# Decode attention with heads in quads: three 64 KB ring tiles, V in 64 KB descriptors, wo in 4 KB descriptors

## The chip, the cores and the metric

The kernel runs on one core of one Trainium2 chip. The metric is the device time of one execution in microseconds. It was 667.13 us before (median of 3 runs, 666.98 to 667.53). On one core an execution counts as slow when it is over 1.5% above the fastest of its kernel. The profile's span (first to last instruction on the core) is about 1.8 us shorter than the device time.

## The reference, cut to what matters

A batch of two rows, each with one token. Attention has 32 heads over a cache of 8192 positions with 128 elements, and a small gated MLP follows.

```python
B, Sq, D = 2, 1, 512
Hq, Hkv, Sk, Dh = 32, 32, 8192, 128          # all bfloat16
q = (layernorm(x) @ wq).reshape(B, Sq, Hq, Dh)
p = softmax(einsum(q, k_cache) * Dh ** -0.5)
h = x + einsum(p, v_cache).reshape(B, Sq, Hq * Dh) @ wo
# the MLP (F = 1376): layernorm(h), W_gate, W_up, relu(gate) * up, W_down
out = h + mlp(layernorm(h))
```

K and V are 134 MB each. With wq, wo and the MLP's weights 281 MB must come from HBM, each byte once.

## The kernel before

It takes two heads at a time (a pair). A partition holds 128 positions of one head, so one K or V tile of a pair has rows of 32 KB, and a ring of six such tiles (buffers used in turn) holds K, V and the weights. VectorE (DVE) multiplies K by q and folds the 128 products to a score; ScalarE (ACT) takes the exponential into `pm`; TensorE (PE) multiplies `pm` with V.

```python
ring = ctx.enter_context(tc.tile_pool(name="ring", bufs=6))
...
def load(cache, n, cuts=(0, T2)):                 # T2 = 128 positions per partition
    b, i = seq[n]
    src = cache[b, 2 * i:2 * i + 2].rearrange("h s d -> (h s) d").rearrange(
        "(p t) d -> p t d", p=P)
    t = ring.tile([P, T2, Dh], bf16, tag="s", name="kv")
    for lo, hi in zip(cuts[:-1], cuts[1:]):
        nc.sync.dma_start(out=t[:, lo:hi, :], in_=src[:, lo:hi, :])
    return t
...
def scores(n, between=None):
    ...
    nc.vector.tensor_tensor(out=kt, in0=kt, in1=qb, op=ALU.mult)             # L177
    while width > 8:                                                          # 128 -> 8
        nc.vector.tensor_tensor(out=..., in0=..., in1=..., op=ALU.add)        # L183
    nc.vector.tensor_reduce(out=sc, ...)                                      # L191
    for half in range(2):
        nc.scalar.activation(out=pm[ps, :, half], in_=sc[ps, :], func=ACT.Exp, ...)
...
load_k(0)
for n in range(N - 2):                            # N = 32 pairs
    load_k(n + 1)
    load_v(n)
    scores(n, between=first_row if n == NP + 2 else None)
    ...
    weighted_v_moving(n)

load_k(N - 1)
wo_sb = ring.tile([P, Hq, D], bf16, tag="s")
nc.sync.dma_start(out=wo_sb, in_=A_wo.rearrange("(h d) n -> d h n", d=P))    # 1 KB rows
load_v(N - 2)
CUTS = (0, T2 // 2, T2 * 7 // 8, T2)
load_v(N - 1, CUTS)
...                                               # gate, up and down weights follow, last of all
```

The softmax here doesn't subtract the row's maximum and nothing guards it: scores larger than these inputs give would overflow.

## Time and profile before

| before | |
|---|---|
| device time | 667.13 us |
| DMA queue q1 | 99.1% of 16 engines' span |
| DVE busy | 90% |
| PE busy | 50% |
| DVE waiting for K | 26.9 us |

The page of the profile, kernel before. Part 1 is busy time by engine. In part 2 the span is cut into 40 slices: DMA is the busy share in tenths, GB/s what was moved. Then come the queue (part 3), the chain that ended last (part 4), and the two costliest groups (part 5: line, engine, operation, shapes, count, busy us, mean ns, idle time before them and its cause).

```profile
span 665.2 us, 4281 instructions
PE 335.7 (50%) x1806; PEld 148.1 (22%) x1806; DVE 597.6 (90%) x224; ACT 51.2 (8%) x171; POOL 1.8 (0%) x12
...
DMA  9999999999999999999999999999999999999996
GB/s 378 439 421 433 439 424 429 437 430 424 437 435 420 437 432 422 437 433 427 431 437 423 432 435 432 427 437 428 427 437 426 430 434 431 426 438 421 376 410 242
...
q1 hardware_dynamic: 15368, 281.06, 99.1%
...
DMA 53%; DVE 44%; issue 1%; PE 1%; SPq 0%; DVEq 0%
...
L177 DVE TENSOR_TENSOR kv<-kv,qrep 128x16384 bf16<-128x16384 bf16 x32 | 278.0, 8689 | 26.9 <-DMA kv<-in_A_k_cache_dram 26.9
L183 DVE TENSOR_TENSOR kv<-kv 128x8192 bf16<-128x8192 bf16 (+3 forms) x128 | 276.2, 2158 | 4.3
```

The queue is hardly ever idle: no slice but the last is below 90%. The chain gives DVE 44%, which by itself leaves open which of the two is the bound: in the first third (from 23 to 210 us) the chain runs over DVE because K has already landed when DVE comes to it. DVE needs 18.7 us for a pair (8.69 + 8.7 of folds + 1.22, and the small gaps between them), DMA about 19.4 us, so DVE has 4% to spare.

The next line is from the DMA view of the kernel before, cut to the stretch from 620 to 626 us, in which nothing but wo moves, in 1 KB packets.

```profile
DMA packets 2038, 2.09 MB, mean 348 GB/s; under 512 B 0, under 2 KB 2038, under 8 KB 2038
```

348 GB/s is 20% below the 430 of the K and V stretches. The packet records of the trace say why. A packet in these records has the size of one contiguous run of its DMA (wq and the rows of K and V, all but the last V, are 8192 packets of 32768 bytes), and a median of 16 of them are in flight, as many as the engines by which the page counts; "descriptor", the word of the title, stands here for one such run. These are median durations over all packets of a size; the column "left over" takes off bytes x 0.03674 ns (the slope from 16 to 32 KB, 27.2 bytes per ns, 435 GB/s on 16 engines).

| packet, bytes | median ns | left over, ns |
|---|---|---|
| 1024 | 49 | 11 |
| 2048 | 84 | 9 |
| 2752 | 113 | 12 |
| 4096 | 162 | 12 |
| 12288 | 464 | 13 |
| 16384 | 614 | 12 |
| 32768 | 1216 | 12 |

By these records a packet has a fixed cost: about 12 ns are left over at every size of the table (9 at 2 KB, of which there are only 128 packets). (Packets of 1 KB overlap a little, as q1's share of 108.9% in that view shows, so that their real rate, 348 GB/s, is somewhat better than the 334 that 49 ns gives.)

### The profile page before, as it was taken

How to read it: one execution, taken by the hardware profiler on the slowest of the kernel's cores; microseconds unless marked ns; L12 is line 12 of the kernel's file. 1: busy time of each engine (PE TensorE's matmuls, PEld its weight loads, DVE VectorE, ACT ScalarE, POOL GpSimd, SP SyncE). 2: the span in 40 equal slices, each digit the busy share in tenths (PEclk: the TensorE clock that was granted, in tenths of full speed). 3: DMA queues.
4: the chain of work that ended last, by engine and by line, in shares of the span. 5: the costliest groups of instructions: out<-in, count | busy, mean ns of one | idle time of the engine just before them, and what ended most of it. 6: DMA issues, size and time to landing. Idle time of an engine off the chain costs nothing.

```text
span 665.2 us, 4281 instructions
## 1 busy us (share of the span) xinstructions
PE 335.7 (50%) x1806; PEld 148.1 (22%) x1806; DVE 597.6 (90%) x224; ACT 51.2 (8%) x171; POOL 1.8 (0%) x12
## 2 busy tenths in 40 slices
PE   3343455654446655444565444556653456654345
PEld 2111122211212221121222111222221122211244
DVE  1699999999999999999999999999999998999931
ACT  2200000000000000000000000000000000000000
POOL 1000000000000000000000000000000000000000
PEclk9757878765787776668877666787666777666755
DMA  9999999999999999999999999999999999999996
GB/s 378 439 421 433 439 424 429 437 430 424 437 435 420 437 432 422 437 433 427 431 437 423 432 435 432 427 437 428 427 437 426 430 434 431 426 438 421 376 410 242
DMA packets 15399, 281.33 MB, mean 423 GB/s; under 512 B 1202, under 2 KB 5396, under 8 KB 6932
## 3 DMA queue, kind: packets, MB, share of 16 engines
q1 hardware_dynamic: 15368, 281.06, 99.1%
q8 instruction: 14, 0.23, 0.1%
q14 instruction: 5, 0.04, 0.0%
q10 hardware_dynamic: 12, 0.00, 0.0%
HBM read 281.05 MB, written 0.00 MB: 422 GB/s over the span
## 4 chain that ended last, share of the span: by engine, by line
DMA 53%; DVE 44%; issue 1%; PE 1%; SPq 0%; DVEq 0%
DMA kv<-in_A_k_cache_dram 45%; DVE kv L183 21%; DVE kv L177 21%; DMA kv<-in_A_v_cache_dram 6%; DVE sc L191 3%; DMA wd_sb<-in_B_W_down_dram 2%; PE o_a L223 1%; SPq L266 0%; PE y_ps L351 0%; SPq L95 0%; PE yt_ps L359 0%; DVEq L191 0%; DVE y_row L362 0%; DVE zi_229 L232 0%; DVE oc L236 0%
## 5 line engine op out<-in xcount | busy, mean ns | idle before, releaser
L177 DVE TENSOR_TENSOR kv<-kv,qrep 128x16384 bf16<-128x16384 bf16 x32 | 278.0, 8689 | 26.9 <-DMA kv<-in_A_k_cache_dram 26.9
L183 DVE TENSOR_TENSOR kv<-kv 128x8192 bf16<-128x8192 bf16 (+3 forms) x128 | 276.2, 2158 | 4.3
L211 PE MATMUL o<-kv,pm_85 128*8 128x512 bf16 x320 | 94.0, 466 | 97.9 <-DMA kv<-in_A_v_cache_dram 77.1
L211 PE MATMUL o<-kv,pm_87 128*8 128x512 bf16 x320 | 91.3, 456 | 87.4 <-DMA kv<-in_A_v_cache_dram 87.4
L211 PE MATMUL o<-kv,pm_86 128*8 128x512 bf16 x320 | 90.2, 452 | 83.6 <-DMA kv<-in_A_v_cache_dram 83.6
L211 PEld LDWEIGHTS <-pm_85 128*8 128x8 bf16 x320 | 32.1, 101 | 156.0 <-issue 102.1
L211 PEld LDWEIGHTS <-pm_87 128*8 128x8 bf16 x320 | 31.7, 99 | 142.8 <-issue 105.4
L211 PEld LDWEIGHTS <-pm_86 128*8 128x8 bf16 x320 | 31.6, 99 | 138.0 <-issue 97.0
L215 ACT ACTIVATE osb<-o 8x512 f32<-8x512 f32 x30 | 17.6, 586 | 498.1 <-PE o L211 498.1
L191 DVE TENSOR_REDUCE sc<-kv 128x128 f32<-128x1024 bf16 x32 | 39.0, 1220 | 3.9 <-DVE kv L183 1.0
L217 PE MATMUL ob_226<-sel,osb 8*128 8x2 f32 x128 | 16.8, 248 | 11.8 <-ACT osb L215 11.8
L217 PE MATMUL ob_227<-sel,osb 8*128 8x2 f32 x112 | 14.7, 249 | 10.3 <-ACT osb L215 10.3
L217 PEld LDWEIGHTS ob_226<-sel,osb 8*128 8x128 f32 x128 | 15.4, 186 | 19.9 <-ACT osb L215 18.6
L217 PEld LDWEIGHTS ob_227<-sel,osb 8*128 8x128 f32 x112 | 13.5, 186 | 17.4 <-ACT osb L215 17.4
L145 PE MATMUL qps<-wq_sb,xnb 128*64 128x512 bf16 x64 | 8.6, 433 | 4.7 <-DMA wq_sb<-in_A_wq_dram 4.7
L196 ACT ACTIVATE pm_86<-sc 64x128 bf16<-64x128 f32 x22 | 7.6, 345 | 33.6 <-DVE sc L191 33.3
L196 ACT ACTIVATE pm_85<-sc 64x128 bf16<-64x128 f32 x22 | 7.6, 344 | 28.8 <-DVE sc L191 28.5
L277 PE MATMUL a_ps<-oc,wo_sb 128*128 128x2 bf16 x128 | 3.9, 165 | 10.7 <-DMA wo_sb<-in_A_wo_dram 10.5
L223 PEld LDWEIGHTS <-kv 128*128 128x128 bf16 x256 | 7.1, 104 | 4.4 <-DMA kv<-in_A_v_cache_dram 4.4
L196 ACT ACTIVATE pm_87<-sc 64x128 bf16<-64x128 f32 x20 | 6.9, 345 | 12.8 <-DVE sc L191 12.4
L145 PEld LDWEIGHTS <-xnb 128*64 128x64 bf16 x64 | 5.0, 122 | 7.9 <-issue 4.7
L236 DVE SCALAR_TENSOR_TENSOR oc<-o_b,zi_230 128x2 bf16<-128x2 f32 x1 | 0.2, 161 | 6.8 <-PE o_b L223 6.8
(73 smaller groups left out, 57.0 us busy)
## 6 DMA issues: line engine op xcount, KB each, us to landing
kv<-in_A_k_cache_dram SPq DMA_DIRECT2D x32, 4096.0 KB, 39.5
kv<-in_A_v_cache_dram SPq DMA_DIRECT2D x31, 4096.0 KB, 48.7
wq_sb<-in_A_wq_dram SPq DMA_DIRECT2D x1, 4096.0 KB, 12.3
wo_sb<-in_A_wo_dram SPq DMA_DIRECT2D x1, 4096.0 KB, 50.8
kv<-in_A_v_cache_dram SPq DMA_DIRECT2D x1, 2048.0 KB, 20.8
kv<-in_A_v_cache_dram SPq DMA_DIRECT2D x1, 1536.0 KB
wgu<-in_B_W_gate_dram SPq DMA_DIRECT2D x1, 1376.0 KB, 27.5
wgu<-in_B_W_up_dram SPq DMA_DIRECT2D x1, 1376.0 KB, 30.6
```

Of the source, the lines that this page charges most:

```text
L145: nc.tensor.matmul(out=qps[half * HALF:(half + 1) * HALF], lhsT=xnb[:, c, b, :], rhs=wq_v[:, c, g * QP:(g + 1) * QP, half, :], start=(c == ...
L177: nc.vector.tensor_tensor(out=kt, in0=kt, in1=qb, op=ALU.mult)
L183: nc.vector.tensor_tensor(out=_view(kt, 0, [[Dh, T2], [1, half]]), in0=_view(kt, 0, [[Dh, T2], [1, half]]), in1=_view(kt, half, [[Dh, T2], ...
L191: nc.vector.tensor_reduce(out=sc, in_=_view(kt, 0, [[Dh, T2], [1, 8]]), axis=AXIS.X, op=ALU.add)
L196: nc.scalar.activation(out=pm[ps, :, half], in_=sc[ps, :], func=ACT.Exp, accum_out=zm[ps, b, i, half:half + 1], scale=SCALE)
L211: nc.tensor.matmul(out=o, lhsT=pm[:, ts, :].rearrange("p t two -> p (t two)"), rhs=vt[:, ts, :].rearrange("p t d -> p (t d)"), start=(g == ...
L215: nc.scalar.activation(out=osb, in_=o, func=ACT.Copy)
L217: nc.tensor.matmul(out=ob[b][:, i, :], lhsT=osb[:, j, :], rhs=sel[:, j, :], start=(j == 0), stop=(j == TG - 1))
L223: nc.tensor.matmul(out=o, lhsT=vt[:, t, :], rhs=pm[:, t, :], start=(t == 0), stop=(t == T2 - 1))
L236: nc.vector.scalar_tensor_tensor(out=oc[:, s:e, :, b], in0=o, scalar=1.0 / D, in1=zi[b][:, s:e, :], op0=ALU.mult, op1=ALU.mult)
L277: nc.tensor.matmul(out=a_ps[:, c, :], lhsT=wo_sb[:, h, c * P:(c + 1) * P], rhs=oc[:, h // 2, h % 2, :], start=(h == 0 and c == 0), stop=(h ...
```

## The change

The intent is larger descriptors for the same bytes. Four heads (a quad) share a tile of 64 KB per partition; V comes in one DMA with 64 KB rows. K still comes in two halves of 32 KB rows, so that DVE can begin with the first. The ring becomes three tiles of twice the size. A head now lies over 32 partitions. The order of wo's rows is also changed: (i p j) with four neighbouring rows on one partition gives 4 KB runs, but then o must have that order too. So o is replicated over partitions by a matmul, and a mask with a sum over the free axis picks each partition's four elements (`gather`). The last quad keeps the old order, and 1 KB rows of wo. The output is turned to two rows and sent in one DMA.

```diff
-    NP = Hq // 2
-    T2 = 2 * Sk // P
+    G = 4
+    NQ = Hq // G
+    T = G * Sk // P
+    J = 4
-    ring = ctx.enter_context(tc.tile_pool(name="ring", bufs=6))
+    ring = ctx.enter_context(tc.tile_pool(name="ring", bufs=3))
...
     def load_k(n):
-        kts[n] = load(A_k_cache, n)
+        kts[n] = load(A_k_cache, n, (0, HT, T))
-    def load_v(n, *cuts):
+    def load_v(n, cuts=(0, T)):
...
-        for half in range(2):
-            ps = slice(half * HALF, (half + 1) * HALF)
-            nc.scalar.activation(out=pm[ps, :, half], ...)
+        for h in range(G):
+            ps = slice(h * Q, (h + 1) * Q)
+            nc.scalar.activation(out=pm[ps, lo:hi, h], ...)
...
+    def gather(s, e):
+        r = reps[s // HQ][:, 0:e - s, :]
+        nc.vector.tensor_tensor(out=r.rearrange("p i (m j) -> p i m j", j=J), in0=...,
+                                in1=_view(pick, 0, [[0, e - s], [1, Q], [0, J]]), op=ALU.mult)
+        nc.vector.tensor_reduce(out=ou[:, s:e, :],
+                                in_=r.rearrange("p i (m j) -> p i j m", j=J), ...)
...
     load_k(0)
-    for n in range(N - 2):
+    load_v(0)
+    for n in range(N - 1):
         load_k(n + 1)
-        load_v(n)
-        scores(n, between=first_row if n == NP + 2 else None)
+        scores(n, 0, 0, HT, between.get(n))
+        scores(n, 1, HT, T)
+        if n < N - 3:
+            load_v(n + 1)
+        elif n == N - 3:
+            load_v(n + 1, (0, HT, T))
+        ret = weighted_v(n)
...
-    nc.sync.dma_start(out=wo_sb, in_=A_wo.rearrange("(h d) n -> d h n", d=P))
+    nc.sync.dma_start(out=wo_sb.rearrange("p i j n -> p i (j n)"),
+                      in_=A_wo[0:LQ * G * Dh, :].rearrange("(i p j) n -> p i (j n)", p=P, j=J))
+    nc.sync.dma_start(out=wol, in_=A_wo[LQ * G * Dh:, :].rearrange("(h d) n -> d h n", d=P))
...
-    for b, eng in zip(range(B), (nc.sync, nc.scalar)):
-        eng.dma_start(out=out[b].rearrange("s (c m) -> (s c) m", c=KC), in_=y_row[b:P:Q, :])
+    nc.vector.tensor_copy(y_row[:, 0:D // 2], yt_ps[:, 0:D // 2])
+    nc.scalar.activation(out=y_row[:, D // 2:], in_=yt_ps[:, D // 2:], func=ACT.Copy)
+    nc.sync.dma_start(out=out.rearrange("b s d -> (b s) d"), in_=y_row)
```

More of the change, by code (lines that the diff above doesn't have):

```diff
@@ L38 @@
     KC = D // P
-    NP = Hq // 2
-    T2 = 2 * Sk // P
+    G = 4
+    NQ = Hq // G
+    T = G * Sk // P
+    J = 4
     TG = 4
-    HALF = P // 2
     EPS = 1e-5
@@ L50 @@
     LASTW = F - FULL
-    NM = 3
-    Q = P // KC
+    NM = 2
+    Q = P // G
     ENG = mybir.EngineType
-    assert Sq == 1 and Hkv == Hq and D == KC * P and Hq % 8 == 0 and P == Dh
+    assert Sq == 1 and Hkv == Hq and D == KC * P and Hq % (2 * G) == 0 and T % 32 == 0 and P == Dh
     consts = ctx.enter_context(tc.tile_pool(name="consts", bufs=1))
     misc = ctx.enter_context(tc.tile_pool(name="misc", bufs=1))
-    ring = ctx.enter_context(tc.tile_pool(name="ring", bufs=6))
+    ring = ctx.enter_context(tc.tile_pool(name="ring", bufs=3))
     spool = ctx.enter_context(tc.tile_pool(name="spool", bufs=2))
@@ L67 @@
     mean_f = consts.tile([P, P], f32)
-    zm = consts.tile([P, B, NP, 2], f32)
+    zm = consts.tile([P, B, 3, NQ - 1], f32)
+    zl = consts.tile([P, B, 3, G], f32)
     eps_t = consts.tile([P, 1], f32)
-    pms = [consts.tile([P, T2, 2], bf16, name=f"pm{i}") for i in range(NM)]
-    sel = consts.tile([2 * TG, TG, 2], f32)
+    pms = [consts.tile([P, T, G], bf16, name=f"pm{i}") for i in range(NM)]
     nc.vector.memset(eps_t, EPS)
@@ L74 @@
     nc.vector.memset(zm, 0.0)
+    nc.vector.memset(zl, 0.0)
     for pm in pms:
         nc.gpsimd.memset(pm, 0.0)
-    y = consts.tile([P, KC, Q], bf16)
-    nc.gpsimd.memset(y, 0.0)
     ident = consts.tile([P, P], bf16)
     masks.make_identity(nc, ident)
-    nc.gpsimd.memset(sel, 0.0)
-    nc.gpsimd.affine_select(out=sel, in_=sel, compare_op=ALU.not_equal, fill=1.0, base=0,
-                            pattern=[[-2, TG], [-1, 2]], channel_multiplier=1)
+    head_of = consts.tile([G * TG, G, Q], f32)
+    nc.gpsimd.memset(head_of, 0.0)
+    for t in range(TG):
+        nc.gpsimd.affine_select(out=head_of, in_=head_of, compare_op=ALU.not_equal, fill=1.0,
+                                base=-G * t, pattern=[[-1, G], [0, Q]], channel_multiplier=1)
+    turn_of = consts.tile([G * TG, TG], f32)
+    nc.gpsimd.memset(turn_of, 1.0)
+    same = consts.tile([P, G, Q], f32)
+    nc.gpsimd.memset(same, 1.0)
+    for t, pat, n in ((turn_of, [[G, TG]], G), (same, [[Q, G], [0, Q]], Q)):
+        neg = [[-s_, c_] for s_, c_ in pat]
+        nc.gpsimd.affine_select(out=t, in_=t, compare_op=ALU.is_ge, fill=0.0, base=0,
+                                pattern=neg, channel_multiplier=1)
+        nc.gpsimd.affine_select(out=t, in_=t, compare_op=ALU.is_ge, fill=0.0, base=n - 1,
+                                pattern=pat, channel_multiplier=-1)
+    pick = consts.tile([P, Q], f32)
+    nc.vector.tensor_reduce(out=pick, in_=ident.rearrange("p (h m) -> p m h", h=G),
+                            axis=AXIS.X, op=ALU.add)
     ctx.enter_context(tc.manual_schedule(engines={ENG.PE, ENG.DVE, ENG.Activation, ENG.SP}))
@@ L93 @@
     nc.scalar.dma_start(out=x_row, in_=A_x.rearrange("b s d -> (b s) d"))
-    wq_sb = ring.tile([P, KC, Hq * Dh], bf16, tag="s")
+    RING = T * Dh
+    wq_sb = ring.tile([P, RING], bf16, tag="s", name="wq_sb")[:, 0:KC * Hq * Dh].rearrange(
+        "p (c n) -> p c n", c=KC)
     nc.sync.dma_start(out=wq_sb, in_=A_wq.rearrange("(p c) n -> p c n", p=P))
@@ L131, with load @@
                             op=ALU.mult)
-    xnb = opool.tile([P, KC, B, HALF], bf16, tag="row")
-    nc.vector.tensor_copy(xnb, xn.unsqueeze(3).to_broadcast([P, KC, B, HALF]))
+    xnb = opool.tile([P, KC, B, Q], bf16, tag="row")
+    nc.vector.tensor_copy(xnb, xn.unsqueeze(3).to_broadcast([P, KC, B, Q]))
     nc.scalar.activation(out=warm, in_=xn[0:1, 0, 0:1], func=ACT.Exp)
-    qrep = consts.tile([P, B, NP, Dh], bf16)
+    qrep = consts.tile([P, B, NQ, Dh], bf16)
     QP = 4
-    wq_v = wq_sb.rearrange("p c (i two d) -> p c i two d", two=2, d=Dh)
+    wq_v = wq_sb.rearrange("p c (i h d) -> p c i h d", h=G, d=Dh)
     for b in range(B):
-        for g in range(NP // QP):
+        for g in range(0, NQ, QP):
             qps = ps_mm.tile([P, QP, Dh], f32, tag="mm", name="qps")
-            for half in range(2):
+            for h in range(G):
                 for c in range(KC):
                     nc.tensor.matmul(
-                        out=qps[half * HALF:(half + 1) * HALF],
+                        out=qps[h * Q:(h + 1) * Q],
                         lhsT=xnb[:, c, b, :],
-                        rhs=wq_v[:, c, g * QP:(g + 1) * QP, half, :],
+                        rhs=wq_v[:, c, g:g + QP, h, :],
                         start=(c == 0), stop=(c == KC - 1),
                     )
-            nc.scalar.activation(out=qrep[:, b, g * QP:(g + 1) * QP, :], in_=qps, func=ACT.Copy)
-    seq = [(b, i) for b in range(B) for i in range(NP)]
+            nc.scalar.activation(out=qrep[:, b, g:g + QP, :], in_=qps, func=ACT.Copy)
+    seq = [(b, i) for b in range(B) for i in range(NQ)]
     N = len(seq)
+    HT = T // 2
+    LQ = NQ - 1
     kts, vts = {}, {}
-    def load(cache, n, cuts=(0, T2)):
+    def load(cache, n, cuts):
         b, i = seq[n]
-        src = cache[b, 2 * i:2 * i + 2].rearrange("h s d -> (h s) d").rearrange(
+        src = cache[b, G * i:G * i + G].rearrange("h s d -> (h s) d").rearrange(
             "(p t) d -> p t d", p=P)
-        t = ring.tile([P, T2, Dh], bf16, tag="s", name="kv")
+        t = ring.tile([P, T, Dh], bf16, tag="s", name="kv")
         for lo, hi in zip(cuts[:-1], cuts[1:]):
@@ L167, in load_k, with scores @@
     def load_k(n):
-        kts[n] = load(A_k_cache, n)
-    def load_v(n, *cuts):
-        vts[n] = load(A_v_cache, n, *cuts)
-    def scores(n, between=None):
+        kts[n] = load(A_k_cache, n, (0, HT, T))
+    def load_v(n, cuts=(0, T)):
+        vts[n] = load(A_v_cache, n, cuts)
+    def scores(n, k, lo, hi, between=None):
         b, i = seq[n]
-        kt = kts.pop(n)
-        qb = _view(qrep[:, b, i, :], 0, [[0, T2], [1, Dh]])
-        nc.vector.tensor_tensor(out=kt, in0=kt, in1=qb, op=ALU.mult)
+        kt, w = kts[n], hi - lo
+        off = lo * Dh
+        nc.vector.tensor_tensor(out=kt[:, lo:hi, :], in0=kt[:, lo:hi, :],
+                                in1=_view(qrep[:, b, i, :], 0, [[0, w], [1, Dh]]), op=ALU.mult)
         if between is not None:
@@ L183, in scores @@
             nc.vector.tensor_tensor(
-                out=_view(kt, 0, [[Dh, T2], [1, half]]),
-                in0=_view(kt, 0, [[Dh, T2], [1, half]]),
-                in1=_view(kt, half, [[Dh, T2], [1, half]]),
+                out=_view(kt, off, [[Dh, w], [1, half]]),
+                in0=_view(kt, off, [[Dh, w], [1, half]]),
+                in1=_view(kt, off + half, [[Dh, w], [1, half]]),
                 op=ALU.add,
@@ L189, in scores @@
             width = half
-        sc = spool.tile([P, T2], f32, name="sc")
-        nc.vector.tensor_reduce(out=sc, in_=_view(kt, 0, [[Dh, T2], [1, 8]]),
+        sc = spool.tile([P, HT], f32, name="sc")
+        nc.vector.tensor_reduce(out=sc[:, 0:w], in_=_view(kt, off, [[Dh, w], [1, 8]]),
                                 axis=AXIS.X, op=ALU.add)
         pm = pms[n % NM]
-        for half in range(2):
-            ps = slice(half * HALF, (half + 1) * HALF)
-            nc.scalar.activation(out=pm[ps, :, half], in_=sc[ps, :], func=ACT.Exp,
-                                 accum_out=zm[ps, b, i, half:half + 1], scale=SCALE)
@@ L200 @@
-    ob = [ps_acc.tile([P, NP, 2], f32, name=f"ob{b}") for b in range(B)]
-    oc = misc.tile([P, NP, 2, B], bf16)
-    zi = [misc.tile([P, NP, 2], f32, name=f"zi{b}") for b in range(B)]
-    def weighted_v_moving(n):
-        b, i = seq[n]
-        vt, pm = vts.pop(n), pms[n % NM]
-        o = ps_o.tile([2 * TG, TG, Dh], f32, tag="o", name="o")
-        for g in range(T2 // TG):
-            ts = slice(g * TG, (g + 1) * TG)
-            nc.tensor.matmul(out=o, lhsT=pm[:, ts, :].rearrange("p t two -> p (t two)"),
-                             rhs=vt[:, ts, :].rearrange("p t d -> p (t d)"),
-                             start=(g == 0), stop=(g == T2 // TG - 1))
-        osb = opool.tile([2 * TG, TG, Dh], f32, tag="row", name="osb")
-        nc.scalar.activation(out=osb, in_=o, func=ACT.Copy)
-        for j in range(TG):
-            nc.tensor.matmul(out=ob[b][:, i, :], lhsT=osb[:, j, :], rhs=sel[:, j, :],
-                             start=(j == 0), stop=(j == TG - 1))
@@ L220, in weighted_v_stationary @@
-    def weighted_v_stationary(n, o, lo, hi):
+        for h in range(G):
+            ps = slice(h * Q, (h + 1) * Q)
+            nc.scalar.activation(out=pm[ps, lo:hi, h], in_=sc[ps, 0:w], func=ACT.Exp,
+                                 accum_out=(zm[ps, b, k, i:i + 1] if i < LQ
+                                            else zl[ps, b, k, h:h + 1]), scale=SCALE)
+    oc = misc.tile([P, LQ, J, B], bf16)
+    ol = misc.tile([P, G, B], bf16)
+    HQ = NQ // 2
+    ou = misc.tile([P, LQ, J], f32)
@@ new lines, with v_moving, weighted_v @@
+    reps = {}
+    def v_moving(n, o, lo, hi):
+        vt, pm = vts[n], pms[n % NM]
+        for t in range(lo, hi, TG):
+            ts = slice(t, t + TG)
+            nc.tensor.matmul(out=o, lhsT=pm[:, ts, :].rearrange("p t h -> p (t h)"),
+                             rhs=vt[:, ts, :].rearrange("p t d -> p (t d)"),
+                             start=(t == 0), stop=(t == T - TG))
+    def weighted_v(n):
+        b, i = seq[n]
+        o = ps_o.tile([G * TG, TG, Dh], f32, tag="o", name="o")
+        v_moving(n, o, 0, T)
+        osb = opool.tile([G * TG, TG, Dh], f32, tag="row", name="osb")
+        for t in range(TG):
+            nc.scalar.activation(out=osb[:, t, :], in_=o[:, t, :], func=ACT.Copy,
+                                 scale=turn_of[:, t:t + 1])
+        if i == LQ:
+            o_l = ps_s.tile([P, G], f32, tag="st", name="o_l")
+            for t in range(TG):
+                nc.tensor.matmul(out=o_l, lhsT=osb[:, t, :], rhs=head_of[:, :, 0],
+                                 start=(t == 0), stop=(t == TG - 1))
+            ol_f = misc.tile([P, G], f32)
+            nc.scalar.activation(out=ol_f, in_=o_l, func=ACT.Copy)
+            return ol_f
+        if i % HQ == 0:
+            reps[i // HQ] = ps_acc.tile([P, HQ, Dh], f32, tag=f"rep{i // HQ}", name="rep")
+        for t in range(TG):
+            nc.tensor.matmul(out=reps[i // HQ][:, i % HQ, :],
+                             lhsT=head_of.rearrange("k h m -> k (h m)"), rhs=osb[:, t, :],
+                             start=(t == 0), stop=(t == TG - 1))
@@ new lines, in gather @@
+    def gather(s, e):
+        r = reps[s // HQ][:, 0:e - s, :]
+        nc.vector.tensor_tensor(out=r.rearrange("p i (m j) -> p i m j", j=J),
+                                in0=r.rearrange("p i (m j) -> p i m j", j=J),
+                                in1=_view(pick, 0, [[0, e - s], [1, Q], [0, J]]), op=ALU.mult)
+        nc.vector.tensor_reduce(out=ou[:, s:e, :],
+                                in_=r.rearrange("p i (m j) -> p i j m", j=J),
+                                axis=AXIS.X, op=ALU.add)
@@ L221, in weighted_v_stationary, with v_stationary @@
+    def v_stationary(n, o, lo, hi):
         vt, pm = vts[n], pms[n % NM]
@@ L223, in weighted_v_stationary @@
             nc.tensor.matmul(out=o, lhsT=vt[:, t, :], rhs=pm[:, t, :],
-                             start=(t == 0), stop=(t == T2 - 1))
-    def sum_z(b, s, e):
-        zb = ps_s.tile([P, e - s, 2], f32, tag="st", name="zb")
-        nc.tensor.matmul(out=zb, lhsT=mean_f, rhs=zm[:, b, s:e, :], start=True, stop=True)
-        return zb
-    def inverse_z(b, s, e, zb=None):
-        nc.vector.reciprocal(out=zi[b][:, s:e, :], in_=zb or sum_z(b, s, e))
-    def normalize(b, s, e, o):
-        nc.vector.scalar_tensor_tensor(out=oc[:, s:e, :, b], in0=o, scalar=1.0 / D,
-                                       in1=zi[b][:, s:e, :], op0=ALU.mult, op1=ALU.mult)
@@ L239, in first_row, with sum_z, row_z, last_z @@
-    def first_row():
-        inverse_z(0, 0, NP, zb0)
-        normalize(0, 0, NP, ob[0])
+                             start=(t == 0), stop=(t == T - 1))
+    def sum_z(zb, lhsT, z):
+        for k in range(3):
+            nc.tensor.matmul(out=zb, lhsT=lhsT, rhs=z[:, k, :], start=(k == 0), stop=(k == 2))
+        return zb
+    def row_z(b, zb):
+        return sum_z(zb, same.rearrange("p h m -> p (h m)"), zm[:, b])
+    def last_z(b, zb):
+        return sum_z(zb, mean_f, zl[:, b])
+    def z_tile():
+        return ps_s.tile([P, LQ + G], f32, tag="st", name="zb")
@@ new lines, in normalize, with invert_last, normalize_last @@
+    def normalize(b, zb):
+        zi = misc.tile([P, LQ], f32, name=f"zi{b}")
+        nc.vector.reciprocal(out=zi, in_=zb)
+        nc.vector.tensor_tensor(out=oc[:, :, :, b], in0=ou,
+                                in1=zi.unsqueeze(2).to_broadcast([P, LQ, J]), op=ALU.mult)
+    def invert_last(b, zb):
+        zi = misc.tile([P, G], f32, name=f"zil{b}")
+        nc.vector.reciprocal(out=zi, in_=zb)
+        return zi
+    def normalize_last(b, o, zi):
+        nc.vector.scalar_tensor_tensor(out=ol[:, :, b], in0=o, scalar=1.0 / D,
+                                       in1=zi, op0=ALU.mult, op1=ALU.mult)
@@ L243 @@
+    def first_row():
+        gather(HQ, LQ)
+        normalize(0, zb0)
+        zil = invert_last(0, zl0)
+        normalize_last(0, ol_f, zil)
+    between = {HQ + 1: lambda: gather(0, HQ), NQ + 1: first_row,
+               NQ + HQ + 1: lambda: gather(0, HQ)}
     load_k(0)
-    for n in range(N - 2):
+    load_v(0)
+    for n in range(N - 1):
         load_k(n + 1)
-        load_v(n)
-        scores(n, between=first_row if n == NP + 2 else None)
-        if n == NP + 1:
-            zb0 = sum_z(0, 0, NP)
-        weighted_v_moving(n)
@@ L253 @@
-    load_k(N - 1)
-    wo_sb = ring.tile([P, Hq, D], bf16, tag="s")
-    nc.sync.dma_start(out=wo_sb, in_=A_wo.rearrange("(h d) n -> d h n", d=P))
-    load_v(N - 2)
-    CUTS = (0, T2 // 2, T2 * 7 // 8, T2)
+        scores(n, 0, 0, HT, between.get(n))
[5 more added lines that the diff above has]
+        ret = weighted_v(n)
+        if n == NQ - 1:
+            ol_f = ret
+            z0 = z_tile()
+            zb0, zl0 = row_z(0, z0[:, 0:LQ]), last_z(0, z0[:, LQ:])
@@ new lines @@
+    W = ring.tile([P, RING], bf16, tag="s", name="W")
+    wo_sb = W[:, 0:LQ * J * D].rearrange("p (i j n) -> p i j n", j=J, n=D)
+    at = LQ * J * D
+    wol = W[:, at:at + G * D].rearrange("p (h n) -> p h n", n=D)
+    at += G * D
+    wgu = W[:, at:at + 2 * KC * F].rearrange("p (g c n) -> p g c n", c=KC, n=F)
+    at += 2 * KC * F
+    wd_sb = W[:, at:at + NF * D].rearrange("p (f n) -> p f n", n=D)
+    nc.sync.dma_start(out=wo_sb.rearrange("p i j n -> p i (j n)"),
+                      in_=A_wo[0:LQ * G * Dh, :].rearrange("(i p j) n -> p i (j n)", p=P, j=J))
@@ L258 @@
+    nc.sync.dma_start(out=wol, in_=A_wo[LQ * G * Dh:, :].rearrange("(h d) n -> d h n", d=P))
+    CUTS = (0, HT, T * 13 // 16, T * 15 // 16, T)
     load_v(N - 1, CUTS)
-    wgu = ring.tile([P, 2, KC, F], bf16, tag="s")
     for g, w in enumerate((B_W_gate, B_W_up)):
         nc.sync.dma_start(out=wgu[:, g], in_=w.rearrange("(c p) n -> p c n", p=P))
-    wd_sb = ring.tile([P, FC, D], bf16, tag="s")
+    wd_l = misc.tile([P, D], bf16)
     blocks = [(f, min(4, NF - f)) for f in range(0, NF, 4)]
@@ L268, with project @@
             in_=B_W_down[f * P:(f + r) * P, :].rearrange("(p r) n -> p (r n)", r=r))
-    nc.sync.dma_start(out=wd_sb[0:LASTW, NF, :], in_=B_W_down[FULL:F, :])
+    nc.sync.dma_start(out=wd_l[0:LASTW, :], in_=B_W_down[FULL:F, :])
     a_ps = ps_acc.tile([P, KC, B], f32)
-    def project_o(s, e):
-        for h in range(2 * s, 2 * e):
-            for c in range(KC):
-                nc.tensor.matmul(
-                    out=a_ps[:, c, :], lhsT=wo_sb[:, h, c * P:(c + 1) * P],
-                    rhs=oc[:, h // 2, h % 2, :],
-                    start=(h == 0 and c == 0), stop=(h == Hq - 1),
-                    skip_group_check=True,
-                )
+    def project(w, o, first=False, last=False):
+        for c in range(KC):
+            nc.tensor.matmul(out=a_ps[:, c, :], lhsT=w[:, c * P:(c + 1) * P], rhs=o,
+                             start=(first and c == 0), stop=last, skip_group_check=True)
     L = B - 1
-    scores(N - 2)
+    zb1 = row_z(L, z_tile()[:, 0:LQ])
     def most_of_last_row():
-        inverse_z(L, 0, NP - 1)
-        normalize(L, 0, NP - 2, ob[L][:, 0:NP - 2, :])
-    scores(N - 1, between=most_of_last_row)
-    project_o(0, NP - 2)
-    zb1 = sum_z(L, NP - 1, NP)
-    inverse_z(L, NP - 1, NP, zb1)
-    o_a = ps_o.tile([P, 1, 2], f32, tag="o", name="o_a")
-    weighted_v_stationary(N - 2, o_a[:, 0, :], 0, T2)
-    normalize(L, NP - 2, NP - 1, o_a)
-    o_b = ps_o.tile([P, 1, 2], f32, tag="o", name="o_b")
-    weighted_v_stationary(N - 1, o_b[:, 0, :], CUTS[0], CUTS[1])
-    project_o(NP - 2, NP - 1)
-    for lo, hi in zip(CUTS[1:-1], CUTS[2:]):
-        weighted_v_stationary(N - 1, o_b[:, 0, :], lo, hi)
-    normalize(L, NP - 1, NP, o_b)
-    project_o(NP - 1, NP)
+        gather(HQ, LQ)
+        normalize(L, zb1)
+    scores(N - 1, 0, 0, HT)
+    scores(N - 1, 1, HT, CUTS[2], most_of_last_row)
+    scores(N - 1, 2, CUTS[2], T)
+    for i in range(LQ):
+        for j in range(J):
+            project(wo_sb[:, i, j, :], oc[:, i, j, :], first=(i == 0 and j == 0))
+    o_b = ps_o.tile([P, G], f32, tag="o", name="o_b")
+    v_stationary(N - 1, o_b, 0, CUTS[2])
+    zil = invert_last(L, last_z(L, z_tile()[:, 0:G]))
+    v_stationary(N - 1, o_b, CUTS[2], T)
+    normalize_last(L, o_b, zil)
+    for h in range(G):
+        project(wol[:, h, :], ol[:, h, :], last=(h == G - 1))
     hc = misc.tile([P, KC, B], f32)
@@ L350 @@
         for c in range(KC):
-            nc.tensor.matmul(out=y_ps[:, c, :], lhsT=wd_sb[0:w, fc, c * P:(c + 1) * P],
+            nc.tensor.matmul(out=y_ps[:, c, :], lhsT=(wd_sb[:, fc] if fc < NF else wd_l[0:w])[:, c * P:(c + 1) * P],
                              rhs=act[0:w, fc, :],
@@ L354 @@
                              skip_group_check=True)
-    nc.vector.tensor_tensor(out=y[:, :, 0:B], in0=y_ps, in1=hc, op=ALU.add)
-    yt_ps = ps_o.tile([P, P], f32, tag="o")
+    y = misc.tile([P, KC, B], bf16)
+    nc.vector.tensor_tensor(out=y, in0=y_ps, in1=hc, op=ALU.add)
+    yt_ps = ps_o.tile([B, D], f32, tag="o")
     for c in range(KC):
-        nc.tensor.matmul(out=yt_ps[c * Q:(c + 1) * Q, :], lhsT=y[:, c, :], rhs=ident,
-                         start=True, stop=True, skip_group_check=True)
-    y_row = misc.tile([P, P], bf16)
-    nc.vector.tensor_copy(y_row, yt_ps)
-    for b, eng in zip(range(B), (nc.sync, nc.scalar)):
-        eng.dma_start(out=out[b].rearrange("s (c m) -> (s c) m", c=KC), in_=y_row[b:P:Q, :])
+        nc.tensor.matmul(out=yt_ps[:, c * P:(c + 1) * P], lhsT=y[:, c, :], rhs=ident,
+                         start=True, stop=True)
+    y_row = opool.tile([B, D], bf16, tag="row")
+    nc.vector.tensor_copy(y_row[:, 0:D // 2], yt_ps[:, 0:D // 2])
+    nc.scalar.activation(out=y_row[:, D // 2:], in_=yt_ps[:, D // 2:], func=ACT.Copy)
+    nc.sync.dma_start(out=out.rearrange("b s d -> (b s) d"), in_=y_row)
 _INS = ['A_x', 'A_k_cache', 'A_v_cache', 'A_wq', 'A_wo', 'B_x', 'B_W_gate', 'B_W_up', 'B_W_down']
```

## The prediction

> **What bounds the kernel now.** The DMA queue. Part 3 of the profile gives queue q1 99.1% of the time of 16 engines, and part 2 shows 420 to 439 GB/s in nearly every slice, so 281 MB take about 660 of the 665 us. DVE is a close second: 90% busy, 18.7 us for each pair of heads (one multiply 8.69, four folds 8.7, one reduce 1.22) against about 19.4 us of DMA for the pair's 8.39 MB of K and V. The table of waits has only 26.9 us of DVE waiting for K, of which 13 at the start. The chain of waits is 53% DMA, 44% DVE: DVE work up to 210 us, then DMA to the end.
>
> **What the change does to DMA.** Median durations of DMA packets in the trace: 1 KB 49 ns, 4 KB 162, 12 KB 464, 16 KB 614, 32 KB 1216. The slope from 16 to 32 KB is 0.0367 ns per byte on one engine (435 GB/s on 16), and what is left over is about 12 ns per packet at 4, 12, 16 and 32 KB. [...]
> - V in 64 KB: 14 quads become 1792 packets where 3584 were. 1792 x 12 ns / 16 = 1.3 us less. K stays at 32 KB (halves), the cut last V about as before: 0.
> - wo: 7/8 of it in 4 KB. The windows of DMA show 348 GB/s while 1 KB wo rows move, so 4.19 MB took 12.05 us; by 162 ns for 4 KB it takes about 10.5. 1.5 to 1.9 us less.
> Nothing else lightens the queue: the bytes are the same.
>
> **What it moves.** DVE keeps the same instruction sizes (half a quad is a pair), plus three gathers and a normalisation, some 3 us in all, inside slack of about 0.7 us a pair. PE streams the same matmuls and is 50% busy. ACT gets four exps of 32 partitions instead of two of 64 and four copies instead of one: ACT is 8% busy. The ring has the same bytes but three slots. I estimate from the durations above: V of the next quad is issued when the second half's reduce ends, with about 9 us (one half of K) still queued; K after that is issued once PE has finished the quad, about 18 us ahead. So the queue should not run dry. At the end DVE finishes the last scores about when the last V lands; compute has about 3 us of slack there before the MLP weights land (waits of 1.3 and 1.4 us for gate and up weights now).
>
> **On the critical path:** the DMA saving, nearly all of it, since the queue is never idle. 667.1 - 1.3 - 1.7 = 664.1 us. I expect 664.1, range 662.0 to 666.5. Faster by over 2%: 0.03; within 2%: 0.93; slower by over 2%: 0.04.
>
> **What would show it:** V packets of 65536 bytes at about 2420 ns; wo stretch at about 400 GB/s; q1 share still 98 to 100%; steady GB/s up by about 0.25%; DVE waits for K of similar total; the end still led by wd. PE, ACT off the chain.
>
> **What would make it wrong:** 64 KB rows split back into smaller packets or slower per byte; K halves (32 KB out of every 64) slower; dips in the GB/s line where three slots leave the queue empty (DVE waits on K above 40 us); DVE, with less than 4% slack, becoming the bound; last scores finishing after the last V so that the tail after the weights grows.

## The result

The changed kernel takes 664.16 us (664.06 to 664.40, 4 runs), beside 667.26 us for the kernel before (4 runs): ratio 0.9954, 95% interval 0.9937 to 0.9971. It is 3.1 us faster, within 2%. A ratio is the mean time of one kernel's fast runs over that of the other's of the same rounds, so not quite the ratio of the quoted medians.

The same lines of the page, for the changed kernel:

```profile
span 662.3 us, 4237 instructions
PE 294.8 (45%) x1704; PEld 131.6 (20%) x1704; DVE 602.6 (91%) x241; ACT 85.8 (13%) x335; POOL 4.7 (1%) x19
...
DMA  9999999999999999999999999999999999999996
GB/s 380 443 443 411 461 394 446 431 445 439 408 432 431 443 414 458 423 416 447 415 453 418 425 451 419 441 423 457 400 439 431 426 453 410 433 433 423 414 413 244
...
q1 hardware_dynamic: 10676, 281.06, 98.9%
...
DVE 45%; DMA 41%; PE 8%; SPq 3%; ACT 2%; issue 1%; DVEq 0%; ACTq 0%
...
L197 DVE TENSOR_TENSOR kv<-kv,qrep 128x16384 bf16<-128x16384 bf16 (+2 forms) x33 | 278.1, 8427 | 31.9 <-DMA kv<-in_A_k_cache_dram 31.9
L204 DVE TENSOR_TENSOR kv<-kv 128x8192 bf16<-128x8192 bf16 (+5 forms) x132 | 276.8, 2097 | 4.4
```

The queue is as full as before, with the same 281.06 MB in 10676 packets instead of 15368. The GB/s line swings more; I take that for the coarser grain: sixteen 64 KB packets, 1 MB, are in flight together and end in bursts (from 35 to 55 us, in half microseconds, the changed kernel's rate goes between 0 and 1835 GB/s; with V in 32 KB, below, the line is between 412 and 443 again, the first and last slice apart). DVE's work on the scores is the same; the gathers and the rest make it 5 us busier, where the prediction had 3, and it waits 5 us more for K. Neither costs time that can be seen: the variant below with both packet changes undone has the same DVE work and waits 33.9 us for K, at the time of the kernel before. In the packet records the 1792 V packets of 65536 bytes have a median of 2421 ns, where two of 32 KB had 2432.

The chain (DVE 45%, DMA 41%) does not name the bound by itself; the experiments do. PE, the issuing queue and ACT now appear on it. That is not a stall. The chain goes back from a landing to whatever released its issue, and K is now issued when PE frees a slot of the ring (15 issues waited for PE). The page's part 6 (issues: KB each, median us from issue to landing) shows 31.9 us for a 4 MB half of K that takes 9.7 us to move, so K was waiting in a queue that had work.

```profile
kv<-in_A_k_cache_dram SPq DMA_DIRECT2D x32, 4096.0 KB, 31.9
```

In the DMA view from 617 to 623 us of the changed kernel, wo moves in 4 KB packets (a few 1 KB ones belong to the last quad's part):

```profile
DMA packets 615, 2.45 MB, mean 408 GB/s; under 512 B 4, under 2 KB 22, under 8 KB 615
```

408 GB/s replace 348. How far ahead of the kernel before is the queue at equal bytes? Counting the bytes of ended packets: 1.1 us at 260 MB (V alone; wo has not begun), 2.6 us at 268 MB (wo almost done), and 2.7 us when the last packet of weights ends (660.53 us before, 657.79 after). So V gave about 1.1 us, wo about 1.5.

### The profile page after: what moved, and what is told of

It reads as the page before. It is cut to its first block, busy times and chain, and to the rows that moved or that the text cites. A ratio compares the mean times of both kernels' runs of the same rounds, so it can differ in the third digit from the quotient of the medians.

```text
span 662.3 us, 4237 instructions
## 1 busy us (share of the span) xinstructions
PE 294.8 (45%) x1704; PEld 131.6 (20%) x1704; DVE 602.6 (91%) x241; ACT 85.8 (13%) x335; POOL 4.7 (1%) x19
## 3 DMA queue, kind: packets, MB, share of 16 engines
q1 hardware_dynamic: 10676, 281.06, 98.9%
## 4 chain that ended last, share of the span: by engine, by line
DVE 45%; DMA 41%; PE 8%; SPq 3%; ACT 2%; issue 1%; DVEq 0%; ACTq 0%
DMA kv<-in_A_k_cache_dram 34%; DVE kv L204 21%; DVE kv L197 21%; PE o L234 6%; DMA W<-in_A_wo_dram 3%; SPq L353 3%; DVE sc L212 3%; DMA W<-in_B_W_down_dram 2%; DMA wq_sb<-in_A_wq_dram 2%; ACT pm L217 2%; PE qps L162 1%; DVE ou L268 0%; DVE rep L265 0%; PE yt_ps L440 0%; PE y_ps L432 0%
## 5 line engine op out<-in xcount | busy, mean ns | idle before, releaser
L234 PE MATMUL o<-kv,pm 128*16 128x512 bf16 x960 | 247.2, 423 | 324.1 <-DMA kv<-in_A_v_cache_dram 281.9
L197 DVE TENSOR_TENSOR kv<-kv,qrep 128x16384 bf16<-128x16384 bf16 (+2 forms) x33 | 278.1, 8427 | 31.9 <-DMA kv<-in_A_k_cache_dram 31.9
L204 DVE TENSOR_TENSOR kv<-kv 128x8192 bf16<-128x8192 bf16 (+5 forms) x132 | 276.8, 2097 | 4.4
L234 PEld LDWEIGHTS <-pm 128*16 128x16 bf16 x960 | 91.5, 97 | 475.4 <-issue 297.1
L217 ACT ACTIVATE pm<-sc 32x128 bf16<-32x128 f32 (+2 forms) x132 | 62.7, 475 | 435.5 <-DVE sc L212 434.0
L212 DVE TENSOR_REDUCE sc<-kv 128x128 f32<-128x1024 bf16 (+2 forms) x33 | 39.2, 1188 | 3.3
L217 ACT ACTIVATION_READ_ACCUMULATOR pm<-sc 32x1 f32 x132 | 32.4, 245 | 0.0
L244 ACT ACTIVATE osb<-o,turn_of 16x128 f32<-16x128 f32 x60 | 16.6, 347 | 112.8 <-PE o L234 105.6
L258 PE MATMUL rep<-osb,head_of 16*128 16x128 f32 x112 | 17.2, 292 | 7.2 <-ACT osb L244 7.2
L258 PEld LDWEIGHTS rep<-osb,head_of 16*128 16x128 f32 x112 | 14.5, 183 | 14.2 <-ACT osb L244 13.1
## 6 DMA issues: line engine op xcount, KB each, us to landing
kv<-in_A_k_cache_dram SPq DMA_DIRECT2D x32, 4096.0 KB, 31.9
```

Of the source, the lines that this page charges most:

```text
L197: nc.vector.tensor_tensor(out=kt[:, lo:hi, :], in0=kt[:, lo:hi, :], in1=_view(qrep[:, b, i, :], 0, [[0, w], [1, Dh]]), op=ALU.mult)
L204: nc.vector.tensor_tensor(out=_view(kt, off, [[Dh, w], [1, half]]), in0=_view(kt, off, [[Dh, w], [1, half]]), in1=_view(kt, off + half, [[ ...
L212: nc.vector.tensor_reduce(out=sc[:, 0:w], in_=_view(kt, off, [[Dh, w], [1, 8]]), axis=AXIS.X, op=ALU.add)
L217: nc.scalar.activation(out=pm[ps, lo:hi, h], in_=sc[ps, 0:w], func=ACT.Exp, accum_out=(zm[ps, b, k, i:i + 1] if i < LQ else zl[ps, b, k, h ...
L234: nc.tensor.matmul(out=o, lhsT=pm[:, ts, :].rearrange("p t h -> p (t h)"), rhs=vt[:, ts, :].rearrange("p t d -> p (t d)"), start=(t == 0), ...
L244: nc.scalar.activation(out=osb[:, t, :], in_=o[:, t, :], func=ACT.Copy, scale=turn_of[:, t:t + 1])
```

## The experiments

All variants start from the changed kernel. The variants ran in three calls on different chips; the kernel before ran in each and had 667.17, 667.29 and 667.28 us, so the calls can be compared. Besides the device time the table has the mean span of the runs and the end of the last weight packet in the profiled run, a single execution. These two are worth having: the variants with more V DMAs have 2.1 us between span and device time, the changed kernel 1.7 to 1.8. Those 0.35 us lie outside what the profile shows and have no cause here.

| kernel | median us | mean span us | last weight packet ends, us | ratio to before (95%) |
|---|---|---|---|---|
| before (first experiments) | 667.17 | 665.40 | 660.53 | 1 |
| changed kernel | 664.16 | 662.48 | 657.79 | 0.9954 (0.9937 to 0.9971) |
| the same again | 664.09 | 662.36 | 657.69 | 0.9953 (0.9941 to 0.9966) |
| wo in 1 KB | 665.87 | 664.14 | 659.41 | 0.9980 (0.9967 to 0.9993) |
| V in 32 KB | 665.86 | 663.80 | 658.89 | 0.9981 (0.9969 to 0.9993) |
| both undone | 667.35 | 665.22 | 660.62 | 1.0002 (0.9990 to 1.0014) |
| V in 16 KB | 668.15 | 666.08 | 661.55 | 1.0014 (1.0001 to 1.0027) |
| V by even and odd partitions, 64 KB | 664.83 | 662.66 | 657.91 | 0.9963 (0.9949 to 0.9977) |
| V by partition halves, 64 KB (fast runs) | 1080.9 | 1078.3 | not compared | 1.6192 (1.6139 to 1.6245) |
| gate, up in 11 KB | 664.91 | 663.16 | 657.42 | 0.9965 (0.9952 to 0.9977) |
| the same, last K earlier | 664.47 | 662.76 | 657.29 | 0.9960 (0.9946 to 0.9974) |
| last K earlier alone | 664.18 | 662.40 | 657.74 | 0.9954 (0.9941 to 0.9966) |
| half of V (wrong result) | 643.59 | 641.88 | not compared | 0.9646 (0.9633 to 0.9659) |
| K in 64 KB | 692.16 | 690.65 | not compared | 1.0377 (1.0360 to 1.0393) |

The expectations speak of semaphore packets: in the packet records of both kernels 16 packets of 4 bytes, 9 ns each, come with every DMA of K, V or weights (976 for 61 of them in the changed kernel).

My theory: the gain is the number of packets times 12 ns. The rivals: the structure (quads, ring, output) or the number of DMAs.

### Undoing wo, V, and both

```diff
-    nc.sync.dma_start(out=wo_sb.rearrange("p i j n -> p i (j n)"),
-                      in_=A_wo[0:LQ * G * Dh, :].rearrange("(i p j) n -> p i (j n)", p=P, j=J))
+    for j in range(J):
+        nc.sync.dma_start(out=wo_sb[:, :, j, :], in_=A_wo[0:LQ * G * Dh, :].rearrange(
+            "(i p j) n -> p i j n", p=P, j=J)[:, :, j, :])
```

> The changed kernel, but the 3584 rows of wo that came in 4 KB packets come again in 1 KB packets (same bytes, same places, four DMAs). Packet theory (what costs is the number of packets, about 12 ns each on its engine, because the queue never idles): 1.5 to 1.9 us slower than the changed kernel, so about 665.9, and 1 to 1.5 us faster than the kernel before. Rival (the gain comes from the quads, the ring and the shorter end, not from packets): within 0.3 us of the changed kernel, 664.2.

```diff
-    def load_v(n, cuts=(0, T)):
+    def load_v(n, cuts=(0, HT, T)):
```

> The changed kernel, but each full V comes in two DMAs of 32 KB packets (as K does). Packet theory: 1792 packets of 12 ns more on 16 engines, 1.3 us slower than the changed kernel, plus about 0.1 us for 14 more sets of semaphore packets of 9 ns: about 665.6. Rival: within 0.3 us of the changed kernel.

Both edits together:

> Both undone: V in 32 KB and wo in 1 KB packets, the rest of the change kept (quads, ring of three, gather, heads over 32 partitions, the new output). Packet theory: the two add, 2.9 to 3.4 us slower than the changed kernel, 667.1 to 667.6, so within 0.4 us of the kernel before. Rival (structure): still 2 us or more faster than the kernel before.

Here and below a variant is set against the mean of the two rows of the changed kernel. The span rises by 1.7 us for wo, 1.4 us for V and 2.8 us for both; the end of the last weight packet by 1.7, 1.1 and 2.9 us. With 2688, 1792 and 4480 packets more that is 10 to 12 ns for each, on one of 16 engines. The kernel with both undone is the kernel before in time (ratio 1.0002) and keeps all the rest of the change. So the quads, the gather, the ring of three and the new output together neither cost nor gain anything that can be measured; the structural rival falls. In device time V in 32 KB cost 1.7 us, a little over its expectation, and 0.3 of it are the time outside the span.

### A larger dose

```diff
-    def load_v(n, cuts=(0, T)):
+    def load_v(n, cuts=(0, T // 4, HT, 3 * T // 4, T)):
```

> The changed kernel with each full V in four DMAs of 16 KB packets: the dose of the undone V change raised. Packet theory: 5376 packets more x 12 ns / 16 = 4.0 us, plus 0.4 us for 42 more sets of semaphore packets: 668.5, three times what V in 32 KB cost (1.7 us measured, so up to 669.3 by that), and slower than the kernel before. If instead 64 KB packets alone are special (a step between 32 and 64 KB), it stays near V in 32 KB: 666.

Four times as many V packets: the span rises by 3.7 us, the last weight packet ends 3.8 us later, and the device time is above the kernel before. 3.7 us x 16 engines / 5376 packets is 11 ns a packet, the semaphore packets included. So 64 KB is not special; the cost follows the count.

### As many DMAs, as few packets: a failed try and a good one

```diff
-            nc.sync.dma_start(out=t[:, lo:hi, :], in_=src[:, lo:hi, :])
+            for ps in ((slice(0, P // 2), slice(P // 2, P)) if hi - lo == T else (slice(0, P),)):
+                nc.sync.dma_start(out=t[ps, lo:hi, :], in_=src[ps, lo:hi, :])
```

> The changed kernel, but each full V comes in two DMAs by partition halves, 64 KB packets as before. As many DMAs as with V in 32 KB, as few packets as in the changed kernel. Packet theory: only the 14 more sets of semaphore packets, 0.1 us, so 664.3. Rival (what costs is the number of DMAs, their starts and completions, not the packets): as slow as V in 32 KB, about 665.6.

It took 1081 us in its three fast runs (1074 to 1086); three more, up to 1128, count as slow (the median of all six is the time near 1090 us that is named below). The profile is of one of the slow runs, 1113 us; a gap of 4% between the runs does not bear on the factors of two that follow. Neither theory had this in view. The DMA view from 35 to 55 us, while V of the first quad moves; first this variant, then the changed kernel over the same time:

```profile
DMA packets 80, 4.19 MB, mean 210 GB/s; under 512 B 16, under 2 KB 16, under 8 KB 16
```

```profile
DMA packets 175, 8.36 MB, mean 418 GB/s; under 512 B 16, under 2 KB 16, under 8 KB 16
```

Half the rate, and a 64 KB packet takes a median of 5139 ns instead of 2421, with 16 packets in flight in both by the packet records. Why is not shown; what the run has is that two DMAs, one into partitions 0 to 63 and one into 64 to 127, moved the same 64 KB packets at half the rate. The test of the number of DMAs was spoilt by this, so it was done again with every second partition in each DMA:

```diff
+            for ps in ((slice(0, P, 2), slice(1, P, 2)) if hi - lo == T else (slice(0, P),)):
+                nc.sync.dma_start(out=t[ps, lo:hi, :], in_=src[ps, lo:hi, :])
```

> Each full V in two DMAs of 64 KB packets again, but by even and odd partitions[...]. [...] V packets back near 2420 ns and the time near the changed kernel. Then it is also the test that the earlier variant failed to be: packet theory 664.3 to 664.5 (14 more sets of semaphores, 0.1 us); rival (number of DMAs) 665.9, as V in 32 KB. If the time is again near 1090, the failure is one of 64-partition DMAs, or of HBM addresses[...].

The V packets are back at a median of 2421 ns and the time at 664.83 us. So 64 partitions in a DMA are not the trouble by themselves; which 64 they are is, or the HBM addresses that are read at one time, which also differ between the two ways. No run parts these two, so the cause of the half rate stays open. As a test of the number of DMAs: the span is 0.2 us longer than that of the changed kernel and the last weight packet ends 0.2 us later, where V in 32 KB, with the same number of DMAs, has 1.4 and 1.1. In device time it is 0.7 us, of which 0.35 lie outside the span. With the number of DMAs held equal, 1792 packets are thus worth 1.1 us of span, 10 ns each. What counts inside the kernel is packets; a DMA more costs little (0.2 us of span for 14 of them). (By the same measure the three more DMAs of the wo variant are worth 0.15 us at most.)

### A step further by the same rule

Gate and up weights in 11008-byte packets. That needs the model dimension in (p c) order, so the weight slices of wo and down become strided:

```diff
-        nc.sync.dma_start(out=wgu[:, g], in_=w.rearrange("(c p) n -> p c n", p=P))
+        nc.sync.dma_start(out=wgu[:, g], in_=w.rearrange("(p c) n -> p c n", p=P))
...
-            nc.tensor.matmul(out=a_ps[:, c, :], lhsT=w[:, c * P:(c + 1) * P], rhs=o,
+            nc.tensor.matmul(out=a_ps[:, c, :], lhsT=w.rearrange("p (m c) -> p c m", c=KC)[:, c, :], rhs=o,
...
-        nc.tensor.matmul(out=yt_ps[:, c * P:(c + 1) * P], lhsT=y[:, c, :], rhs=ident,
+        nc.tensor.matmul(out=yt_ps.rearrange("b (m c) -> b c m", c=KC)[:, c, :], lhsT=y[:, c, :], rhs=ident,
```

> A step further by the same rule: the gate and up weights in 256 packets of 11008 bytes where 1024 of 2752 were (113 ns each, 12 of it fixed), by keeping the model dimension in (p c) order to the end of the kernel; weight loads of wo and down then stride by 8 bytes. Packet theory: 768 x 12 ns / 16 = 0.6 us less, 663.6, if the strided weight loads at the end cost nothing. Rival (the end of the kernel is bound by its compute, not by the landing of the last weights, or the strided weight loads are slower): 664.2 or more.

The DMA ended 0.3 us earlier, about half of the 0.6 that the rule gives (an 11008-byte packet took 416 ns, four of 2752 bytes 452). The time did not follow: 664.91 us, 0.8 slower. The end of the timeline shows why. Columns: start us, duration us, engine, line, operation and tiles; in brackets the idle time before and what ended it. Kernel before:

```profile
651.08 0.16 DVE L236 SCALAR_TENSOR_TENSOR oc<-o_b,zi_230 128x2 bf16<-128x2 f32 x1 [6.76 <-PE o_b L223]
654.00 1.71 PE L325 MATMUL gate_ps<-hd,wgu 128*96 128x2 bf16 x44 [1.31 <-DMA wgu<-in_B_W_gate_dram]
657.51 1.71 PE L325 MATMUL up_ps<-hd,wgu 128*96 128x2 bf16 x44 [1.37 <-DMA wgu<-in_B_W_up_dram]
...
662.32 0.66 SPq L364 DMA_DIRECT2D out_dram<-y_row  x1
```

Changed kernel:

```profile
650.78 0.17 DVE L305 SCALAR_TENSOR_TENSOR ol<-o_b,zil 128x4 bf16<-128x4 f32 x1 [1.09 <-PE o_b L275]
652.86 1.65 PE L406 MATMUL gate_ps<-hd,W 128*96 128x2 bf16 x44 [0.25 <-DVE hd L392]
654.80 1.72 PE L406 MATMUL up_ps<-hd,W 128*96 128x2 bf16 x44
658.02 0.29 PEld L432 LDWEIGHTS <-W 128*128 128x128 bf16 x8 [0.16 <-DMA W<-in_B_W_down_dram]
658.77 0.58 PE L440 MATMUL yt_ps<-ident,y 128*2 128x128 bf16 x4 [0.26 <-DVE y L437]
659.40 0.41 DVE L443 CAST y_row<-yt_ps 2x256 bf16<-2x256 f32 x1 [0.68 <-PE yt_ps L440]
659.90 0.37 ACT L444 ACTIVATE y_row<-yt_ps 2x256 bf16<-2x256 f32 x1 [11.08 <-DVE y_row L443]
660.30 0.31 SPq L445 DMA_DIRECT2D out_dram<-y_row  x1
```

Gate weights in 11 KB:

```profile
651.20 0.17 DVE L305 SCALAR_TENSOR_TENSOR ol<-o_b,zil 128x4 bf16<-128x4 f32 x1 [1.10 <-PE o_b L275]
657.34 1.47 PE L432 MATMUL y_ps<-act,W 128*128 128x2 bf16 x40 [0.33 <-DVE act L425]
659.20 1.01 PE L440 MATMUL yt_ps<-ident,y 128*2 128x128 bf16 x4 [0.26 <-DVE y L437]
661.16 0.30 SPq L445 DMA_DIRECT2D out_dram<-y_row  x1
```

Before, PE waits 1.31 and 1.37 us for the gate and up weights. In the changed kernel o of the last heads is ready only 0.3 us earlier while the weights land 2.8 us earlier, and those waits are gone; 0.16 us are left before the last of the down weights. With 11 KB packets nothing at the end waits for DMA any more. There o is ready 0.4 us later (the scores that precede it end 0.4 us later; why is not shown), and the strided write of the turned output takes 1.01 us instead of 0.58.

So the next variant also gives the end room: the first half of the last K goes ahead of the second half of the V before it, and the output's order is put right in the copies, not in the matmul.

```diff
+        for lo, hi in ((0, HT), (HT, T)):          # V of quad N - 2, K of quad N - 1
+            nc.sync.dma_start(out=vts[n][:, lo:hi, :], in_=sv[:, lo:hi, :])
+            nc.sync.dma_start(out=kts[n + 1][:, lo:hi, :], in_=sk[:, lo:hi, :])
...
+    y_o = y_row.rearrange("b (m c) -> b c m", c=KC)
+    y_i = yt_ps.rearrange("b (c m) -> b c m", c=KC)
+    nc.vector.tensor_copy(y_o[:, 0:2], y_i[:, 0:2])
+    nc.scalar.activation(out=y_o[:, 2:], in_=y_i[:, 2:], func=ACT.Copy)
```

> Gate and up weights in 11 KB packets again (that variant ended its DMA 0.4 us earlier, yet was 0.8 us slower: its end was bound by the scores of the last quad and by a strided write of the turned output), now with the first half of the last K sent ahead of the second half of the V before it, so that DVE can start the last quad's scores about 2.4 us earlier, and with the order of the output put right in the copy instead of in the matmul. If the end's compute was what held it: 0.4 to 0.6 us faster than the changed kernel, about 663.6. If something else did: 664.5 or more.

And the earlier K alone, with the packets of the changed kernel:

> Only the earlier last K, packets as in the changed kernel. The bytes, packets and the landing of the last weights are the same, and the changed kernel's end already waits for that landing (0.16 us), so: 664.0 to 664.2, no gain alone. If the changed kernel's end is bound by its compute: 0.3 us or more faster.

The earlier K alone gives 664.18 us: two microseconds more room for compute (o of the last heads is ready to be scaled at 648.62 us, not 650.78), no gain, as expected of an end that waits for DMA. With 11 KB packets and the earlier K it is 664.47 us, 0.4 better than with 11 KB packets alone, but still 0.3 slower than the earlier K alone, run beside it; my 663.6 is missed. The timeline of this last variant:

```profile
658.12 0.17 DVE L451 TENSOR_TENSOR y<-y_ps,hc 128x8 bf16<-128x8 f32 x1 [1.81 <-PE y_ps L446]
658.34 0.59 PE L454 MATMUL yt_ps<-ident,y 128*2 128x128 bf16 x4 [0.26 <-DVE y L451]
658.97 0.71 DVE L459 CAST y_row<-yt_ps 2x256 bf16<-2x256 f32 x1 [0.68 <-PE yt_ps L454]
659.77 0.72 ACT L460 ACTIVATE y_row<-yt_ps 2x256 bf16<-2x256 f32 x1 [13.49 <-DVE y_row L459]
660.52 0.31 SPq L461 DMA_DIRECT2D out_dram<-y_row  x1
```

y is ready at 658.12 us, 0.4 us earlier than in the changed kernel (658.55): most of the rule's 0.6 has arrived. The two strided copies, one after the other, take 0.71 and 0.72 us where the plain ones took 0.41 and 0.37, and give 0.65 us back. No version beats the changed kernel.

### How much more is there

```diff
-    def load_v(n, cuts=(0, T)):
+    def load_v(n, cuts=(0, HT)):
...
-                             rhs=vt[:, ts, :].rearrange("p t d -> p (t d)"),
+                             rhs=vt[:, (vs := slice(t % HT, t % HT + TG) if n < N - 2 else ts), :]...
```

> Wrong result on purpose: only the first half of each full V is loaded and PE reads it twice; 59 MB fewer of 281, all engines' work as before. How much is there to be gained from DMA at all? My estimate: DVE becomes the bound: start 23 us + 32 x 18.7 + gathers 3 + end 15 = 640 us (636 to 648). If DVE had more room than 90% busy suggests, down to the DMA's 530.

With 59 MB fewer (and a wrong result) the time falls to 643.6 us only. From its page, the busy times, the queue and the chain:

```profile
PE 319.8 (50%) x1704; PEld 137.4 (21%) x1704; DVE 601.2 (94%) x241; ACT 85.8 (13%) x335; POOL 4.7 (1%) x19
...
q1 hardware_dynamic: 10676, 222.34, 83.3%
...
DVE 85%; DMA 7%; issue 3%; SPq 3%; PE 1%; DVEq 0%; ACT 0%; ACTq 0%
```

That was expected (636 to 648). DVE is the second bound, about 20 us below: it waits for K only once, 13.5 us at the start. Taking a fifth of the bytes away gives 3%, and then DVE binds. What DMA still costs at the start and the end (7% of this chain) was not tested.

### K in 64 KB as well

```diff
-        kts[n] = load(A_k_cache, n, (0, HT, T))
+        kts[n] = load(A_k_cache, n, (0, T))
```

> K in 64 KB packets too, so one DMA for each K: 2048 packets fewer, by the packet rule 1.5 us less. But DVE must wait for the whole K, and V of the next quad can only be sent when DVE has finished the K in its slot: by my estimate that leaves the queue empty for 1 to 3 us in each quad, and the end 8 us longer. Packet theory alone: 662.5. With the ring's timing: 675 to 700, and a DMA share of q1 below 98%.

```profile
GB/s 410 440 425 422 417 428 368 425 426 421 432 365 459 391 425 364 426 466 440 422 372 425 425 425 426 364 428 437 455 379 425 426 421 428 364 441 372 420 403 70
...
q1 hardware_dynamic: 8372, 281.06, 95.7%
...
L197 DVE TENSOR_TENSOR kv<-kv,qrep 128x16384 bf16<-128x16384 bf16 (+2 forms) x33 | 278.1, 8428 | 61.5 <-DMA kv<-in_A_k_cache_dram 61.5
```

The fewest packets of all, and 692 us. DVE begins each quad only when all of K has landed, so the ring's slots come free later than the queue needs them: the GB/s line dips to between 364 and 379 again and again, and DVE waits 61.5 us. The last slice moves almost nothing (70 GB/s): the end, too, waits for compute (the last weight packet ends at 679.86 us, the output is issued at 689.33). This is the failure that the prediction named as its risk; keeping K in halves is what avoids it.

## Why the prediction was right

- **The bound.** Right: q1 99.1% before and 98.9% after, no slice but the last below 90%, and the time follows the packets when they are put back (1.7, 1.4, 2.8 and 3.7 us of span).
- **V, 1.3 us.** Right: 1.4 us by span when undone, 1.1 us by the bytes and by the end of the last packet, and 1.1 us of span with the number of DMAs held equal. The term is slightly too large: the runs put 10 to 12 ns on a packet, the prediction 12. 64 KB packets last 2421 ns where 2420 was written.
- **wo, 1.5 to 1.9 us.** Right: 1.7 us when undone; the stretch ran at 408 GB/s where about 400 was written.
- **Nothing else.** Right: with both undone the rest of the change is worth 0.2 us of span. Inside the end two things cancel: from the last weight landing to the issue of the output it takes 0.8 us longer (1.31 us before, 2.09 after: a longer turning matmul and two copies in a row), and the single output DMA ends about 0.9 us sooner after its issue (2.0 us to the end of the span, 2.9 before). A landing is here the moment the transfer's semaphore is set. The prediction did not foresee these two; that they cancel is luck, and so is a measured 664.16 this close to 664.1.
- **The queue does not run dry.** Right for K in halves; K in 64 KB shows how near the edge is.
- **PE and ACT off the chain.** Wrong by the letter: they have 8% and 2% of it. They stand there as releasers of a slot whose transfer had to queue anyway. (ACT's busy time went from 51.2 to 85.8 us: an exponential over 32 partitions x 128 elements, written with a stride of 8 bytes, took 483 ns, one over 64 partitions x 128 with a stride of 4 bytes 345; no run tells the stride from the partitions.)
- **About 3 us of compute slack at the end.** Right for the kernel before (waits of 1.31 and 1.37 us), but only just enough: the change used nearly all of it, and 0.16 us of waiting is left at the last weights. The prediction set the slack beside the saving without saying how near they were; that it sufficed is partly luck. For the next step it did not.

## What to carry to other kernels

When a DMA queue is busy all the time, price a descriptor change from the packet records: count of packets saved, times the fixed cost per packet, over the number of engines; here 12 ns by the records and 10 to 12 by the runs, worth 20% of the rate at 1 KB and 0.5% between 32 and 64 KB. Look at once at what the larger piece delays (the slot it frees, the engine that must wait for all of it), because that can cost far more than the packets save (K in 64 KB: 28 us lost for 1.5 us of packets by the rule). And before going on with the same bound, take its load away in one wrong-result run: here it showed 3% before DVE takes over in the body of the kernel. The 11 KB variants show that its end can take over long before that.
